# A dense two-layer block behind attention: eight of its nine remaining feature chunks go in pairs through seven block products in place of eight

## The chip, the cores and the metric

The program runs on one core of a Trainium2 chip. The metric is the device time of one execution in microseconds, the median of several runs. The names of the engines are those of the profile: PE (TensorE), DVE (VectorE), ACT (ScalarE), POOL (GpSimd), SP (SyncE, which here issues every DMA).

## The reference, cut to what matters

```python
scores = scale * np.matmul(q, k.transpose(0, 1, 3, 2))          # 8 x 8 heads, 576 tokens, 64 wide
thresh = np.max(scores, axis=-1, keepdims=True) - tau
scores = np.where(scores >= thresh, scores, -1000000000.0)
attn = np.exp(scores - np.max(scores, axis=-1, keepdims=True))
attn = attn / (np.sum(attn, axis=-1, keepdims=True) + 1e-09)
x = np.matmul(attn, v)              # turned to 4608 tokens x 512
h = x @ w_in                        # 512 -> 2048
g = np.maximum(h, 0.0) + alpha * np.minimum(h, 0.0)
out = g @ w_out                     # 2048 -> 512
```

w_in and w_out arrive as 64-bit floats; the kernel takes them apart on the chip.

## The kernel before, in words

Every float32 operand of a matmul is split in a rounded part ("h") and the rest ("l"), and a product is three matmuls: h by h, h by l, l by h. A split is one ScalarE copy (h) and one subtraction on GpSimd or VectorE (l).

The 2048 features are 16 chunks of 128. While attention runs, the first seven (F1 = 7) are decoded (`Split64`: ScalarE takes the size, VectorE shifts bits, GpSimd or VectorE joins the halves) and applied to groups of 256 tokens between attention's own matmuls; their second-layer sum goes to DRAM (`part`). Attention ends near 850 us. Then three things follow.

1. What is left of the first seven chunks, four groups of 256 tokens, named jobs j0 to j3. `first_layer` (tiles `phj`) does one chunk: 12 matmuls of 256 columns, then `prelu` on VectorE (L228, L229) and `split_g` (ACT L237, POOL L240) into `gj`. `second_layer` (tiles `accj`) does two blocks of 128 tokens with 21 matmuls of 512 columns each. x is split by `fetch_x` (ACT L835, POOL L836).
2. Chunks 7 to 10 for nine groups of 512 tokens, first layer and second layer, 12 and 12 matmuls of 512 columns per chunk and group; VectorE adds the sum to the residual loaded from `part` (L988, tiles `pinj`, `obj`) and it is written to `part` again.
3. Chunks 11 to 15 likewise, written to the output.

The order on an engine is that in which the code calls it (`manual_schedule`); `at_cycle` puts small work into numbered cycles between matmul groups, so that a decode or a split stands so many cycles ahead of its use. An engine runs its queue strictly in that order. PSUM has eight banks: four `ph` and four `acc`.

## Time and profile before

| what | value |
|---|---|
| median of three runs | 1378.01 us (1376.72 to 1378.1) |
| span of the profiled execution | 1374.2 us |
| PE busy | 1332.0 us (97%), 8116 matmuls |
| DVE / ACT / POOL busy | 72% / 61% / 60% |
| granted clock of PE, mean | 0.998 |
| DMA | 186.06 MB, mean 135 GB/s |

The profile is of one execution; its span runs from the first to the last instruction, and the time of a run has a few microseconds around it (1378.01 against 1374.2; the profiled execution's own run time isn't listed apart). Matmuls are pipelined, so their busy times overlap; distances between starts give their price. In a row by groups the columns are the line, the engine, the operation with the tiles written and read, the count, the busy time and mean in ns, then the engine's idle time ahead of them with what ended it.

### The profile page before, as it was taken

What the parts mean: (1) busy time and instruction counts of PE and PEld (TensorE: products, weight loads), DVE (VectorE), ACT (ScalarE), POOL (GpSimd) and SP (SyncE); (2) the same over time, 40 slices, a digit from 0 to 9 for tenths busy, and PEclk for the clock granted to TensorE, in tenths of its full rate; (3) what the DMA queues carried; (4) which work ended last, traced back from release to release, by engine and by line L of the source; (5) the groups of instructions that cost most, each with busy time, mean ns of one, the idle gap of its engine ahead of it and who ended that gap; (6) DMA issues with size and microseconds to landing.
All of it is one profiled execution on the core that took longest, in us unless ns stands there. A gap on an engine that the chain in (4) does not pass through costs nothing.

```text
span 1374.2 us, 24020 instructions
## 1 busy us (share of the span) xinstructions
PE 1332.0 (97%) x8116; PEld 1178.4 (86%) x8116; DVE 989.5 (72%) x1970; ACT 843.4 (61%) x1915; POOL 825.4 (60%) x949
## 2 busy tenths in 40 slices
PE   5988899999999999999999999999999999999998
PEld 4556789999999999999999998898888888888887
DVE  6999988889889889888888883873655644333432
ACT  6888888888888888888888873442323322211110
POOL 4886676576676666666666654884656554433431
PEclk9999999999999999999999999999999999999999
DMA  8643634644544545445445313445556352343222
GB/s 253 175 145 104 184 103 119 167 125 125 160 122 134 148 126 144 136 126 150 136 132 145 115 50 110 131 131 169 167 170 200 122 184 92 109 150 110 93 77 77
DMA packets 115179, 186.06 MB, mean 135 GB/s; under 512 B 18320, under 2 KB 49328, under 8 KB 115056
## 3 DMA queue, kind: packets, MB, share of 16 engines
q1 hardware_dynamic: 115056, 184.52, 45.0%
q8 instruction: 65, 1.06, 0.3%
q14 instruction: 58, 0.48, 0.1%
HBM read 104.41 MB, written 37.90 MB: 104 GB/s over the span
## 4 chain that ended last, share of the span: by engine, by line
PE 86%; ACT 5%; DVE 4%; issue 2%; POOL 2%; DMA 2%; SPq 0%; POOLq 0%; DVEq 0%; ACTq 0%
PE accj L246 19%; PE phj L210 18%; PE s L423 11%; PE av L570 11%; PE acca L246 9%; PE pha L210 9%; PE t L467 7%; PE tk L483 1%; DVE p L458 1%; DVE nmx L438 1%; DMA wri<-in_moe_w_in_dram 1%; ACT xb L583 1%; ACT p L446 1%; ACT xa L581 1%; ACT xh L196 1%
## 5 line engine op out<-in xcount | busy, mean ns | idle before, releaser
L240 POOL TENSOR_TENSOR gj<-ptj,gj 128x512 fp32r<-128x512 f32 (+1 forms) x109 | 129.2, 1187 | 237.2 <-ACT gj L237 236.5
L237 ACT ACTIVATE gj<-ptj 128x512 fp32r<-128x512 f32 (+1 forms) x109 | 62.9, 577 | 338.1 <-DVE ptj L229 338.0
L438 DVE TENSOR_REDUCE nmx<-s 128x1 f32<-128x576 f32 x288 | 217.2, 754 | 71.5 <-PE s L423 68.0
L246 PE MATMUL accj<-wo,gj 128*128 128x512 f32 x1140 | 262.4, 389 | 0.5 <-POOL gj L240 0.5
L246 PEld LDWEIGHTS accj<-wo,gj 128*128 128x128 f32 x1140 | 213.7, 188 | 45.3 <-POOL gj L240 1.0
L210 PE MATMUL phj<-xhj,wi 128*128 128x512 f32 (+1 forms) x816 | 232.7, 366 | 0.0
L458 DVE SCALAR_TENSOR_TENSOR p<-s,thr,p 128x576 f32<-128x576 f32 x256 | 206.9, 808 | 2.8 <-ACT thr L451 2.4
L446 ACT ACTIVATE p<-s,nmx 128x576 f32<-128x576 f32 x256 | 190.2, 743 | 8.2 <-DVE nmx L438 7.7
L246 PE MATMUL acca<-wo,ga 128*128 128x512 f32 x588 | 185.9, 422 | 1.6 <-POOL ga L240 0.8
L423 PE MATMUL s<-kh,qst 128*128 128x288 f32 x640 | 142.4, 313 | 33.6 <-DVE p L458 19.1
L210 PEld LDWEIGHTS phj<-xhj,wi 128*128 128x128 f32 x816 | 147.4, 188 | 25.4
L228 DVE TENSOR_SCALAR ptj<-phj,alpha_sb 128x512 f32<-128x512 f32 (+1 forms) x109 | 74.3, 681 | 124.1 <-PE phj L210 120.2
L210 PE MATMUL pha<-xh,wi 128*128 128x256 f32 x784 | 156.8, 283 | 0.2 <-ACT pra L223 0.2
L467 PE MATMUL t<-ident,p 128*128 128x128 f32 x1024 | 154.7, 274 | 0.0
L210 PE MATMUL phj<-xlj,wi 128*128 128x512 f32 (+1 forms) x408 | 149.8, 367 | 1.1 <-POOL xlj L836 0.9
L423 PEld LDWEIGHTS s<-kh,qst 128*128 128x128 f32 x640 | 101.4, 193 | 57.6 <-issue 25.1
L988 DVE TENSOR_TENSOR obj<-accj,pinj 128x512 f32<-128x512 f32 x72 | 49.8, 692 | 139.5 <-PE accj L246 118.5
L423 PE MATMUL s<-kl,qst 128*128 128x288 f32 x640 | 133.7, 299 | 0.0
L210 PEld LDWEIGHTS pha<-xh,wi 128*128 128x128 f32 x784 | 127.9, 190 | 4.5 <-ACT pra L223 1.5
L467 PEld LDWEIGHTS t<-ident,p 128*128 128x128 f32 x1024 | 126.5, 141 | 0.1
L233 POOL TENSOR_TENSOR pta<-pta,pra 128x256 f32<-128x256 f32 x94 | 69.4, 738 | 74.2 <-ACT pra L223 71.6
L246 PEld LDWEIGHTS acca<-wo,ga 128*128 128x128 f32 x588 | 102.0, 191 | 13.7 <-POOL ga L240 1.3
(130 smaller groups left out, 2867.3 us busy)
## 6 DMA issues: line engine op xcount, KB each, us to landing
pinj<-part SPq DMA_DIRECT2D x72, 256.0 KB
kr<-in_k_dram SPq DMA_DIRECT2D x31, 320.0 KB
rb<-rvd SPq DMA_DIRECT2D x64, 144.0 KB
xs<-xa SPq DMA_DIRECT2D x32, 288.0 KB
part<-obj SPq DMA_DIRECT2D x36, 256.0 KB
out_dram<-obj SPq DMA_DIRECT2D x36, 256.0 KB
vr<-in_v_dram SPq DMA_DIRECT2D x28, 320.0 KB
qr<-in_q_dram SPq DMA_DIRECT2D x31, 288.0 KB
```

The costliest lines, as they stand in the source:

```text
L210: nc.tensor.matmul(ph[:, :n], w[:, c, :], xx[:, c, :n], start=(c == 0 and ti == 0), stop=(c == NCC - 1 and ti == 2),)
L228: nc.vector.tensor_scalar(t[:, :n], ph[:, :n], 0.0, alpha_sb[:, fc : fc + 1], op0=ALU.min, op1=ALU.mult)
L233: nc.gpsimd.tensor_tensor(t[:, :n], t[:, :n], r[:, :n], op=ALU.add)
L237: nc.scalar.activation(g[:, 0, :n], t[:, :n], AF.Copy)
L240: nc.gpsimd.tensor_tensor(g[:, 1, :n], t[:, :n], f(g[:, 0, :n]), op=ALU.subtract)
L246: nc.tensor.matmul(acc[:m, :], gg[:, g, o : o + m], w, start=(first and ti == 0), stop=(last and ti == 2))
L423: nc.tensor.matmul(ps[:, h, :288], w, kk[:, a + h * 288 : a + (h + 1) * 288], start=(ki == 0 and i == 0), stop=(ki == 1 and i == n - 1),)
L438: nc.vector.tensor_reduce(self.nmx[:, j : j + 1], self.S[u][0][:, :, :288], axis=AX.XY, op=ALU.max, negate=True)
L446: nc.scalar.activation(pj, ps[:, :, :288], AF.Exp, bias=nmx[:, j : j + 1], scale=1.0)
L458: nc.vector.scalar_tensor_tensor(pj, ps[:, :, :288], thr[:, j : j + 1], pj, op0=ALU.is_ge, op1=ALU.mult, accum_out=self.sm[:, c : c + 1])
L467: nc.tensor.transpose(tb[:, c, :], pt[:, j, j * D + c * P : j * D + (c + 1) * P], ident)
L570: nc.tensor.matmul(pa[:m, :n], w, x, start=(part == 0 and c == 0), stop=(part == z.parts[-1] and c == NKC))
```

## The change

Chunk 7 stays as it is and becomes "the odd one". Chunks 8 to 15 become four pairs. For a pair, layer one is a 2 x 2 block product (two chunks by two halves of the 512 inputs, times two halves of the inputs by two stretches of 384 tokens), and layer two is one as well (two stretches of 256 tokens by the pair's two chunks, times two chunks by two halves of the 512 outputs). Each is done with seven products of sums of blocks in place of eight products of blocks. The products are numbered 1 to 7.

Layer one goes over all tokens first: six rounds s of 768 tokens, four pairs each, 24 units; a product is 6 matmuls of 384 columns (`product_a`). Sums of x blocks (`xt`, on GpSimd, in round 0 on VectorE) are split once per round; sums of w_in blocks once for all, decoded during part 1. Products 1, 6, 5 and 3 of a unit go to bank X, 7 and 4 to W, 2 to Y, so that a bank holds running sums: it is read between two products (`after_a`). Two chunks by two stretches come out, get the slope and go to DRAM (`gd`). The slope is applied as one maximum; chunks with a slope above one have their sign turned (`turn_sb`). Two units of a round carry the odd chunk's 12 matmuls right behind product 2 (`odd_a`).

Layer two then takes nine blocks s of 512 tokens: the gates of all chunks come back from DRAM, VectorE makes four sums and seven splits of 128 x 1024 columns (`gates_at`), and a product is 24 matmuls of 256 columns (`product_b`); the odd chunk's 24 are added in the same banks, one part in bank Z. `after_b` adds each product's bank to the residual `pin`, which is loaded 8 cycles ahead and lives in one of two memories by turns. w_out is decoded during layer one and its sums are split in the last four units (`weights_b`) into the places of the w_in sums. `turn_over` and `turn_again` give x's memory to the gates.

`ORDER` interleaves a unit's products with those of the unit before; `TURN` does it at the passage from layer one to layer two and `LAST` at the end.

```diff
-    fcs2 = list(range(F1, NF))
+    odd = F1
+    fcs2 = list(range(F1 + 1, NF))
...
+    ORDER = ((0, 1), (1, 5), (0, 7), (0, 2), (0, 6), (1, 3), (0, 4))
+    TURN = ((1, 5), (0, 1), (1, 3), (0, 7), (0, 2), (0, 6), (0, 4))
+    LAST = ((0, 1), (1, 5), (0, 7), (1, 3), (0, 6), (0, 2), (0, 5), (0, 4), (0, 3))
+    BANK = {1: "X", 6: "X", 5: "X", 3: "X", 7: "W", 4: "W", 2: "Y"}
...
+    USE = (1, 7, 2, 6, 4, 5, 3)
+    ODD = (0, 1)
...
+            def done(w):
+                if r == 0:
+                    w32[pr] = mem.lx.tile([P, 2, DM], F32, tag="w32", name=f"w32_{pr}", bufs=2)
+                nc.gpsimd.tensor_tensor(w32[pr][:, r], f(w.t), f(w.low), op=ALU.add)
...
+                tt(st[7], st[1], st[5], op=ALU.subtract)
+                tt(st[6], st[4], st[7], op=ALU.subtract)
...
+                tt(st[5], st[5], st[4], op=ALU.add)
+                tt(st[3], st[2], st[6], op=ALU.subtract)
...
+            at_cycle(c, temps)
+            for k, ns in enumerate(((1, 7, 2), (6, 4))):
+                for n in ns:
+                    at_cycle(c + k, hi, n)
+                    at_cycle(c + k + 1, lo, n, nc.gpsimd if n in (1, 2, 4) else nc.vector)
...
-        decode_part(parts2[0], i + 6, DEC2)
+        c = i + 5
+        for n in range(NJ):
+            first_word(n, c)
+            c += FW
+        odd_word("i", c, 4)
...
+                if k == (GB - F1 - 1 if final else 0) and num > 0 and not (num == 1 and pending.begun):
+                    second_layer(pending, mem.mp1)
...
+                    c += 1 if u < NA else 3
+                    if u < NA and prod == 2 and u % NP in ODD:
+                        steps.append((u, "o"))
+                        start[u, "o"] = c
+                        c += 1
...
+        def psum(u, prod):
+            b = BANK[prod]
+            fresh = prod in (1, 7, 2)
+            if fresh:
+                bank[u, b] = ps_3.tile([P, 512], F32, tag=b, name=f"p{b}{u}", bufs=3 if b == "X" else 2)
+            return bank[u, b], fresh
+
+        def product_a(u, prod):
+            s, pr = divmod(u, NP)
+            ph, fresh = psum(u, prod)
+            w = wsum[pr, prod]
+            xh, xl = xop[s, prod]
+            for c in range(2):
+                wh, wl = (w[:, k, c * P : (c + 1) * P] for k in range(2))
+                for ti, (a, x) in enumerate(((wh, xh), (wh, xl), (wl, xh))):
+                    nc.tensor.matmul(
+                        ph[:, :H1],
+                        a,
+                        x[:, c],
+                        start=(fresh and c == 0 and ti == 0),
+                        stop=(c == 1 and ti == 2),
+                        skip_group_check=not fresh,
...
+            for j, n in enumerate(((1, 2), ("o", 3))[ODD.index(pr)]):
+                xh, xl = xop[s, n]
...
+            if of is None:
+                g = mem.br.tile([P, H1], F32, tag="cr", name=f"cr{u}", bufs=2)
+                copy(g, ph, scale=turn_sb[:, col])
+                at_cycle(i + 1, larger, g, ph, slope_sb)
+            else:
+                g = sv.pop((u, of))
+                whole = ph
+                if prod == 5:
+                    whole = ps_3.tile([P, 512], F32, tag="Z", name=f"pZ{u}")[:, :H1]
+                stt(whole, ph, turn_sb[:, col], g, op0=ALU.mult, op1=ALU.add)
+                at_cycle(i + 1, copy, g, whole)
+                at_cycle(i + 2, larger, g, whole, alpha_sb)
...
+            at_cycle(need[1] - 8, load_pins)
...
+                c = need[n] - 6
+                if s == 0 and n == 2:
+                    c = start[NA - 1, 3] + 1
...
+        def product_b(u, prod):
+            acc, fresh = psum(u, prod)
+            s = u - NA
+            gh, gl = gop[s, prod]
+            todo = [(tb, pr) for tb in range(2) for pr in range(NP)]
+            for n, (tb, pr) in enumerate(todo):
+                wh, wl = (bsum[pr, prod][:, k] for k in range(2))
+                for ti, (g, w) in enumerate(((gh, wh), (gh, wl), (gl, wh))):
+                    nc.tensor.matmul(
+                        acc[:, tb * H2 : (tb + 1) * H2],
+                        g[:, pr, tb * P : (tb + 1) * P],
+                        w,
+                        start=(fresh and n == 0 and ti == 0),
+                        stop=(n == len(todo) - 1 and ti == 2),
+                        skip_group_check=not fresh,
+                    )
+                if n in (3, 6):
+                    cycle()
+            if prod == 7:
+                bank[u, "Z"] = ps_3.tile([P, 512], F32, tag="Z", name=f"pZ{u}")
+                odd_b(s, bank[u, "Z"], 1, 1, True)
+                at_cycle(i + 1, after_b, u, "o")
+            elif prod in (2, 3, 4):
+                odd_b(s, acc, *{2: (0, 0), 3: (0, 1), 4: (1, 0)}[prod], False)
...
+        def after_b(u, prod):
+            s = u - NA
+            acc = bank[u, "Z" if prod == "o" else BANK[prod]].rearrange("p (a m) -> p a m", a=2)
+            h, k = {1: (0, 0), 2: (0, 0), 6: (1, 0), 4: (1, 0), 7: (1, 1), 5: (1, 1), 3: (0, 1), "o": (1, 1)}[prod]
+            dst = pin[s, h][:, :, k * H2 : (k + 1) * H2]
+            nc.vector.tensor_tensor(dst, acc, dst, op=ALU.add)
+            if prod == (3 if h == 0 else 4 if start[u, 4] > start[u, 5] else 5):
+                t0 = G2 * s + H2 * h
+                nc.sync.dma_start(out[t0 : t0 + H2, :].rearrange("(a p) m -> p a m", p=P), pin[s, h])
```

The attention part keeps its instructions. Three places show how the queues change.

GpSimd's queue in part 1, at jobs j1 to j3. Before: gate splits (L240) and a joined weight word (L156) now and then.

```order
L240 TENSOR_TENSOR gj_1_12654<-ptj_1_12651,gj_1_12654 128x256
L240 TENSOR_TENSOR gj_2_12680<-ptj_2_12677,gj_2_12680 128x256
L156 TENSOR_TENSOR wi_12649<-wti_12588,wri_12499 128x512
L240 TENSOR_TENSOR gj_3_12701<-ptj_3_12698,gj_3_12701 128x256
L240 TENSOR_TENSOR gj_4_12721<-ptj_4_12718,gj_4_12721 128x256
L240 TENSOR_TENSOR gj_5_12741<-ptj_5_12738,gj_5_12741 128x256
L240 TENSOR_TENSOR gj_6_12763<-ptj_6_12760,gj_6_12763 128x256
L156 TENSOR_TENSOR wti_12672<-wti_12672,wi_12758 128x512
L240 TENSOR_TENSOR gj_0_12797<-ptj_0_12794,gj_0_12797 128x256
```

After, in the same part: gate splits (now L248) among the word's two steps (L849 rest, L975 join) and the splits of the weight sums (L861, `wa`).

```order
L248 TENSOR_TENSOR gj_4_13050<-ptj_4_13047,gj_4_13050 128x256
L861 TENSOR_TENSOR wa_1_13040<-w_2_12925,wa_1_13040 128x256
L861 TENSOR_TENSOR wa_2_13044<-w_2_12925,wa_2_13044 128x256
L248 TENSOR_TENSOR gj_5_13077<-ptj_5_13074,gj_5_13077 128x256
L861 TENSOR_TENSOR wa_4_13071<-w_2_12925,wa_4_13071 128x256
L248 TENSOR_TENSOR gj_6_13101<-ptj_6_13098,gj_6_13101 128x256
L849 TENSOR_TENSOR wri_12928<-wri_12928 128x512
L248 TENSOR_TENSOR gj_0_13128<-ptj_0_13125,gj_0_13128 128x256
L861 TENSOR_TENSOR wa_5_13117<-w_2_12925,wa_5_13117 128x256
L975 TENSOR_TENSOR w_3_13146<-wti_12991,wri_12928 128x512
```

Between two gate splits now stand up to two weight-sum splits or a word's step, where one word stood in four or five.

VectorE's queue in the same part. Before: activations of two lines per chunk (`ptj` from `phj`) and one step of a word.

```order
L228 TENSOR_SCALAR ptj_6_12760<-phj_6_12744,alpha_sb 128x256
L229 SCALAR_TENSOR_TENSOR ptj_6_12760<-phj_6_12744,ptj_6_12760 128x256
L156 TENSOR_TENSOR wri_12591<-wri_12591 128x512
L228 TENSOR_SCALAR ptj_0_12794<-phj_0_12766,alpha_sb 128x256
L229 SCALAR_TENSOR_TENSOR ptj_0_12794<-phj_0_12766,ptj_0_12794 128x256
L137 TENSOR_SCALAR wto_12781<-wto_12781 128x512
L140 TENSOR_SCALAR wto_12781<-wto_12781 128x512
```

After: the sums of w_in blocks (L993, L994), which read GpSimd's join `w`, stand ahead of a chunk's activation.

```order
L993 TENSOR_TENSOR sum_2_13036<-w_2_12925 128x256
L994 TENSOR_TENSOR sum_2_13037<-w_2_12925,sum_2_13036 128x256
L146 TENSOR_SCALAR wti_12991<-wti_12991 128x512
L236 TENSOR_SCALAR ptj_4_13047<-phj_4_13023,alpha_sb 128x256
L237 SCALAR_TENSOR_TENSOR ptj_4_13047<-phj_4_13023,ptj_4_13047 128x256
L861 TENSOR_TENSOR wa_7_13042<-sum_2_13036,wa_7_13042 128x256
L151 SCALAR_TENSOR_TENSOR wti_12991<-wri_12928,wti_12991 128x512
L236 TENSOR_SCALAR ptj_5_13074<-phj_5_13053,alpha_sb 128x256
L237 SCALAR_TENSOR_TENSOR ptj_5_13074<-phj_5_13053,ptj_5_13074 128x256
L861 TENSOR_TENSOR wa_6_13069<-sum_2_13037,wa_6_13069 128x256
```

The activation of chunk 4 (`ptj_4`) and with it the bank `phj` wait for GpSimd's word `w_2`.

VectorE's queue in the last 200 us. Before, a group of four chunks and its residual additions:

```order
L228 TENSOR_SCALAR ptj_14_15645<-phj_14_15632,alpha_sb 128x512
L229 SCALAR_TENSOR_TENSOR ptj_14_15645<-phj_14_15632,ptj_14_15645 128x512
L228 TENSOR_SCALAR ptj_15_15664<-phj_15_15651,alpha_sb 128x512
L229 SCALAR_TENSOR_TENSOR ptj_15_15664<-phj_15_15651,ptj_15_15664 128x512
L228 TENSOR_SCALAR ptj_11_15695<-phj_11_15670,alpha_sb 128x512
L229 SCALAR_TENSOR_TENSOR ptj_11_15695<-phj_11_15670,ptj_11_15695 128x512
L988 TENSOR_TENSOR obj_0_15717<-accj_0_15701,pinj_0_15586 128x512
L988 TENSOR_TENSOR obj_128_15742<-accj_128_15720,pinj_128_15588 128x512
```

After, half a block of layer two: residual additions (L1524, from banks X, W, Y, Z), splits (L861, `gl`), sums (L1439, L1447).

```order
L861 TENSOR_TENSOR gl_7_17350<-gt_7_17325,gh_7_17349 128x1024
L1524 TENSOR_TENSOR pin_0_17252<-pX_17336,pin_0_17252 128x2x256
L861 TENSOR_TENSOR gl_o<-go_17271,gh_o 128x512
L861 TENSOR_TENSOR gl_2_17382<-gr_01_17173,gh_2_17381 128x1024
L1439 TENSOR_TENSOR gt_6_17396<-gr_11_17186,gt_7_17325 128x1024
L1524 TENSOR_TENSOR pin_1_16993<-pX_17075,pin_1_16993 128x2x256
L861 TENSOR_TENSOR gl_6_17417<-gt_6_17396,gh_6_17416 128x1024
L1447 TENSOR_TENSOR gr_01_17173<-gr_01_17173,gt_6_17396 128x1024
L1524 TENSOR_TENSOR pin_1_17254<-pZ_17438,pin_1_17254 128x2x256
L1524 TENSOR_TENSOR pin_1_17254<-pW_17403,pin_1_17254 128x2x256
L861 TENSOR_TENSOR gl_3_17462<-gr_01_16912,gh_3_17461 128x1024
L1524 TENSOR_TENSOR pin_0_17252<-pY_17448,pin_0_17252 128x2x256
```

The activations are gone from there (they stand in layer one), and operand splits of 1024 columns stand behind additions that wait for a product.

More of the change, by code (lines that the diff above doesn't have):

```diff
@@ L27 @@
 G1 = 256
+H1 = 384
 G2 = 512
@@ L64 @@
 CYCLE = 2.6
+FW = 5
 def f(ap):
@@ new lines, in tile_masked_attention_moe @@
+        left[2].close()
+        mem.xr = pool(2, "xraw", "left")
+        others = x_at(0)
+        puts = second_layer(jobs[-1], mem.ws)
+        p1.close()
+        mem.xe = pool(6, "xe", "left")
+        mem.br = pool(3, "br", "right")
+        mem.pa = pool(4, "pa", "right")
+        others(puts)
+        start = {}
+        steps = []
+        c = i + 1
+        for n in range(NA + NB + 1):
+            for lag, prod in {NA: TURN, NA + NB - 1: LAST, NA + NB: ()}.get(n, ORDER):
+                u = n - lag
+                if 0 <= u < NA + NB:
+                    start[u, prod] = c
+                    steps.append((u, prod))
+                    c += 1 if u < NA else 3
[3 more added lines that the diff above has]
+                        c += 1
@@ new lines, in tile_masked_attention_moe @@
+        begin = start[0, 1]
+        end = c
+        place = {step: n for n, step in enumerate(step for step in steps if step[0] >= NA)}
+        left[5].close()
+        ps_3 = left[5].enter_context(tc.tile_pool(name="ps_3", bufs=1, space=PSUM, reuse_waits="tile"))
+        for s in range(1, NA // NP):
+            x_at(s)
+        bank = {}
+        def psum(u, prod):
[4 more added lines that the diff above has]
+            return bank[u, b], fresh
@@ new lines, in odd_a @@
+        def odd_a(u):
+            s, pr = divmod(u, NP)
+            ph = bank[u, "o"] = ps_3.tile([P, 512], F32, tag="Y", name=f"pO{u}", bufs=2)
+            wh, wl = (wi[odd][:, k].rearrange("p (c f) -> p c f", c=NCC) for k in range(2))
+            for j, n in enumerate(((1, 2), ("o", 3))[ODD.index(pr)]):
+                xh, xl = xop[s, n]
+                for c in range(2):
+                    for ti, (a, x) in enumerate(((wh, xh), (wh, xl), (wl, xh))):
+                        nc.tensor.matmul(
+                            ph[:, :H1],
+                            a[:, 2 * j + c],
+                            x[:, c],
+                            start=(j == 0 and c == 0 and ti == 0),
+                            stop=(j == 1 and c == 1 and ti == 2),
+                        )
@@ L1012, in tile_masked_attention_moe @@
+        for _ in range(3):
+            cycle()
+    for st in reversed(left):
         st.close()
```

440 lines of the change are left out of this document (372 added, 68 removed).

## Prediction

> **What bounds the kernel now.** I read the table by windows first, to see which engine is full in which stage behind attention (850 to 927: what is left of the first seven chunks; from there the nine others).
>
> ```profile
> core 0: us, PE busy (x) PEld busy (x) DVE busy (x) ACT busy (x) POOL busy (x), PEclk, DMA share, GB/s
> 850.00:927.00 77.00, 75.88 (x492) 68.95 (x491) 63.38 (x102) 37.35 (x80) 59.77 (x58) 1.00 0.44 137
> 927.00:1170.00 243.00, 243.00 (x1073) 201.18 (x1073) 125.52 (x187) 67.53 (x117) 137.00 (x104) 1.00 0.48 156
> 1170.00:1370.00 200.00, 199.46 (x881) 164.78 (x880) 70.54 (x100) 34.65 (x59) 75.17 (x59) 1.00 0.32 104
> ```
>
> From 927 on TensorE never stops, its granted clock is 1.00, and every other engine has a third of its time or more to spare. Only fewer or shorter matmuls shorten this part. Between 850 and 927 TensorE is also full, but VectorE has 82% and GpSimd 78% of the window busy: there the cover is thin. Next the price of one matmul, from starts in TensorE's timeline:
>
> ```profile
> 872.21 0.28 PE L210 MATMUL phj<-xhj,wi 128*128 128x256 f32 x1
> ...
> 882.01 9.71 PE L246 MATMUL accj<-wo,gj 128*128 128x512 f32 x42
> ...
> 922.05 9.71 PE L246 MATMUL accj<-wo,gj 128*128 128x512 f32 x42
> ...
> 1331.47 13.76 PE L246 MATMUL accj<-wo,gj 128*128 128x512 f32 x60
> 1345.07 0.39 PE L210 MATMUL phj<-xhj,wi 128*128 128x512 f32 x1
> ```
>
> Sixty matmuls of 512 columns start within 13.60 us: 226.7 ns each. Seven chunks of twelve with 256 columns lie between 872.21 and 882.01: 84 in 9.80 us, 116.7 ns. Each has its own weight load, and the load is hidden at both widths. 384 columns do not occur; halfway is 171.7 ns, which I take (170 by 512's price per column, 175 by 256's).
>
> **TensorE's work.** Nine chunks cost 9 x 9 x 12 = 972 matmuls in layer one and 36 x 9 x 3 = 972 in layer two: 1944 x 226.7 = 440.7 us. After: layer one has 24 units (6 stretches of 768 tokens, 4 pairs) of 7 products of 6 matmuls, 1008, and 12 x 12 = 144 for the ninth chunk, 1152 x 171.7 = 197.8 us. Layer two has 9 blocks of 7 x 24 plus 24, 1728 x 116.7 = 201.7 us. Together 399.5: **41.2 us less**. Seven blocks for eight would save a ninth of it, 49; the narrower matmuls give 8 back. By the Trainium skill (TensorE: Matmul & The Clock Gate, Back-to-back issue gap) a matmul takes N/2.4 + 2.5 ns; the saving would be 43.6 us, an estimate from that page; the rows show 7 to 11 ns more per matmul, so the trace disagrees.
>
> **What the cover costs.** The other engines get sums, splits and more evictions. Their prices, by groups (count | busy, mean ns) and GpSimd's first rows of that stage:
>
> ```profile
> L240 POOL TENSOR_TENSOR gj<-ptj,gj 128x512 fp32r<-128x512 f32 x81 | 105.5, 1302 | 219.0 <-ACT gj L237 219.0
> ...
> L240 POOL TENSOR_TENSOR gj<-ptj,gj 128x256 fp32r<-128x256 f32 x28 | 23.7, 852 | 18.3 <-ACT gj L237 17.5 <-DMA wri<-in_moe_w_in_dram 0.7
> ...
> L156 POOL TENSOR_TENSOR wi<-wti,wri 128x512 fp32r<-128x512 f32 x9 | 12.6, 1402 | 1.3 <-DVE wti L156 1.2
> ...
> L836 POOL TENSOR_TENSOR xlj<-xrj,xhj 128x256 fp32r<-128x256 f32 x12 | 10.8, 920 | 1.7 <-ACT xhj L835 1.6
> ...
> L229 DVE SCALAR_TENSOR_TENSOR ptj<-phj,ptj 128x512 f32<-128x512 f32 x81 | 56.0, 692 | 2.8
> ...
> L229 DVE SCALAR_TENSOR_TENSOR ptj<-phj,ptj 128x256 f32<-128x256 f32 x28 | 11.9, 425 | 1.0
> ...
> L145 DVE SCALAR_TENSOR_TENSOR wto<-wro,wto 128x512 int32<-128x512 int32 x9 | 9.9, 1101 | 0.1
> ...
> L156 DVE TENSOR_TENSOR wri<-wri 128x512 f32<-128x512 f32 x9 | 7.2, 805 | 0.0
> ...
> L988 DVE TENSOR_TENSOR obj<-accj,pinj 128x512 f32<-128x512 f32 x72 | 49.8, 692 | 139.5 <-PE accj L246 118.5 <-DMA out_dram<-obj 16.2 <-DMA pinj<-part 2.7
> ...
> L341 DVE TENSOR_TENSOR kl<-kr,kh 128x640 fp32r<-128x640 f32 x1 | 0.8, 825 | 0.0
> L341 DVE TENSOR_TENSOR kl<-kr,kh 128x576 fp32r<-128x576 f32 x1 | 0.8, 759 | 0.0
> ...
> L237 ACT ACTIVATE gj<-ptj 128x512 fp32r<-128x512 f32 x81 | 51.2, 632 | 311.6 <-DVE ptj L229 311.6
> ...
> L196 ACT ACTIVATE xh<-xr 128x1024 fp32r<-128x1024 f32 x1 | 1.0, 1046 | 0.0
> ...
> 852.44 0.73 POOL L240 TENSOR_TENSOR gj<-ptj,gj 128x256 fp32r<-128x256 f32 x1 [6.04 <-ACT gj L237]
> 853.88 0.74 POOL L240 TENSOR_TENSOR gj<-ptj,gj 128x256 fp32r<-128x256 f32 x1 [0.71 <-ACT gj L237]
> 855.32 0.73 POOL L240 TENSOR_TENSOR gj<-ptj,gj 128x256 fp32r<-128x256 f32 x1 [0.70 <-ACT gj L237]
> 856.77 0.75 POOL L240 TENSOR_TENSOR gj<-ptj,gj 128x256 fp32r<-128x256 f32 x1 [0.72 <-DMA wri<-in_moe_w_in_dram]
> ```
>
> *Seven chunks' remainder* (to 927). GpSimd now has 28 gate splits (0.85), 12 splits of x (0.92), 8 rests, 8 joins and 3 of the ninth chunk at 1.40, and 16 splits of weight sums at the 256-column price 0.85: 23.9 + 11.0 + 26.6 + 13.6 = 75.1 us, in order. From its first at 852.44, with the 2.1 us that it waits between the first four in any case, the last gate split ends at 929.6. TensorE wants it 18 matmuls into the last second layer. That one stands at 922.05, behind a first chunk of twelve (2.7 us) that no longer stands there: 919.3 + 4.1 = 923.4. So GpSimd is 6 us late without a wait in mid-queue; and there are such waits, since VectorE's sums stand behind GpSimd's join, the next chunks' activations behind the sums, and with four banks TensorE's next chunk behind those. At GpSimd's undisturbed 0.73 for a split and 1.3 for a word the total is 66 us and it is just in time: 0. With both queues waiting in turn, up to 18. I take **10**, nearest to the means of that window.
>
> *Into layer one's stage.* Its x loads (1.5 MB) stand behind the last first-layer chunk, under a second layer of 9.5 us (42 matmuls); at the 156 GB/s of the window above they take 9.8 us and product 1 needs only the first quarter, so that is about covered; product 4's split stands late in GpSimd's queue: 1.5 (0 to 4).
>
> *Layer one's stage.* A round (4 units, 768 tokens) gives TensorE 192 matmuls, 33.0 us. GpSimd: 20 half operands of 384 columns at 1.08 (between 0.85 and 1.30) and two words of 2.8, 27.4. VectorE: 30 evictions of 384 at 0.56, two sums at 0.96 (825 ns for 640 and 1.03 ns for each of 128 columns more), two words of some 3.1 (1.1 and 0.8 by L145 and L156, two shorter ones), 25. ScalarE: 30 copies at about 0.52 (632 ns for 512 columns), 8 splits of 768 at about 0.84 (half way to 1.05 for 1024), words, 25. All fit; in order, with three products (3.1 us) between an eviction and the next product in its bank. I take 4 us of waits in six rounds (0 to 12).
>
> *Turn to layer two.* Product 2's operand of the first block and the second block's loads can start only at layer one's last product, one 3.5 us product ahead of use: 2 (0 to 5).
>
> *Layer two's stage.* A block gives TensorE 192 matmuls, 22.4 us. VectorE: 7 splits and 4 sums of 1024 columns, each 825 + 384 x 1.03 = 1.22, 13.4; 8 additions at 0.69, 5.5; the ninth's split 0.7: 19.6, or 88%. The residual's tile is loaded only after the output of two blocks earlier has left it, so the block's first addition waits about 2.7 us by my count (19.7 us in, the write's 2.9, two 512 KB loads ahead of it, its own). What is queued behind on VectorE are operand splits with 2.6 us of slack. ScalarE has 8 us of work. DMA moves 4.5 MB a block, 199 GB/s, where the window above had 156 at a share of 0.48. I take 4 us for nine blocks (0 to 15).
>
> *The end.* The last addition was followed by a 256 KB write:
>
> ```profile
> 1370.61 0.69 DVE L988 TENSOR_TENSOR obj<-accj,pinj 128x512 f32<-128x512 f32 x1 [2.71 <-PE accj L246]
> 1371.33 0.33 SPq L990 DMA_DIRECT2D out_dram<-obj  x1
> ```
>
> 2.9 us from the issue to the span's end at 1374.2. Now it is 512 KB: 1.5 more (0 to 3).
>
> **Sum**: -41.2 + 10 + 1.5 + 4 + 2 + 4 + 1.5 = -18.2. The span of the profiled execution is 1374.2, the median of the runs 1378.01, so 3.8 us lie around the span and stay. 1356.0 span, **1360 us**. All lower ends: 1337; all upper: 1394.
>
> **Rivals.**
> *Everything is hidden* (0.22). The queues catch up, only the end and a few us remain: 1340. For it: 100% TensorE in the last two windows. Against: GpSimd's 75 us in a stage of 71.
>
> *VectorE becomes layer two's bound* (0.10), slower. If its 1024-column operations take twice L156's 805 ns, 1.61, a block is 17.7 + 5.5 + 0.8 = 24.0, and with the residual wait 26.7: 9 x 4.3 = 39 in place of 4, 1395. It turns slower when a block passes 22.4 + 22/9 = 24.8 us. For: 805 ns for 512 columns against 0.69 by the quiet rows. Against: GpSimd, which was busy beside L156, has nothing to do in that stage.
>
> *GpSimd becomes layer one's bound* (0.13). VectorE's operations on two SBUF operands (words' sign and join at 1.10 and 0.81, two sums at 0.96, weight sums 1) are 6.7 us of a round; if GpSimd stands still meanwhile its round is 34.1 against 33.0, and with 2.5 us of waits in order 36.6: 6 x 3.6 = 22 for 4, 1378; half of it, 1368. For: a 256-column split took 0.73 at 852.44 and 0.85 in the mean, beside VectorE's words. Against: most of VectorE's work there reads PSUM. By the Trainium skill (SBUF — State Buffer, Who interferes with whom) a VectorE operation with two SBUF inputs and a GpSimd one that reads SBUF exclude each other, the second waiting out the first; the trace's 0.73 against 0.85 agrees in kind.
>
> *Narrow matmuls cost more* (0.05), slower. If layer two's 256-column ones took 140 ns because of their loads, 1728 x 23.3 = 40: 1400. It decides at 129.4 (22 us over 1728). Against: the 84 in a row at 116.7; the most any row here shows is 120 (84 between 849.26 and 859.33).
>
> ```profile
> 849.26 0.28 PE L210 MATMUL phj<-xh,wi 128*128 128x256 f32 x1
> ...
> 859.33 0.28 PE L210 MATMUL phj<-xhj,wi 128*128 128x256 f32 x1
> ```
>
> **Numbers.** The forecast, TensorE bound with some 23 us of new waits, has 0.50, and by itself 1350 to 1370. Leaving out under 0.2 above and little below, the range is 1337 to 1382. About 0.2% (2.8 us) is what a measurement can tell here. Faster: 0.50 + 0.22 + most of GpSimd's 0.13 = 0.81; same 0.05 out of that case's upper end; slower 0.14.
>
> **What would show it.** Starts of layer-one products 1.03 us apart and of layer-two products 2.8 (with the ninth 3.5) show the price. TensorE's idle time behind GpSimd and VectorE between 860 and 940 shows the first term; idle time with VectorE as releaser in the last 200 us the fifth. I am wrong if layer one begins by 930, if a layer-two block takes over 24 us, or if the narrow matmuls' starts lie more than 125 ns apart.

## The result, and the profile after

The changed kernel takes 1391.35 us (median of four runs, 1391.04 to 1392.61), beside it the kernel before 1377.9: a ratio of 1.0105, 95% interval 1.0091 to 1.012. It is some 13 to 14 us slower, where the forecast was 18 us faster. Its profiled execution spans 1389.3 us.

TensorE does have less to do. Its timeline gives the two new prices by the starts of whole products, and the first and last start of each stage:

```profile
850.27 0.28 PE L218 MATMUL phj<-xh,wi 128*128 128x256 f32 x1
...
945.12 0.34 PE L1256 MATMUL pX<-xh,wa 128*128 128x384 f32 x1
...
979.22 0.34 PE L1256 MATMUL pX<-xh,wa 128*128 128x384 f32 x1
...
981.30 0.34 PE L1256 MATMUL pW<-xh,wa 128*128 128x384 f32 x1
...
1169.60 0.28 PE L1502 MATMUL pX<-wb,gh 128*128 128x256 f32 x1
...
1209.66 0.40 PE L1502 MATMUL pW<-wb,gh 128*128 128x256 f32 x2
...
1218.96 0.40 PE L1502 MATMUL pW<-wb,gh 128*128 128x256 f32 x2
...
1384.50 0.28 PE L1485 MATMUL pX<-wo,gl_o 128*128 128x256 f32 x1
```

Twelve matmuls of 384 columns start within 2.08 us, 173.3 ns each; 78 of 256 columns within 9.30 us, 119.2 ns. So the new work is 1152 x 173.3 + 1728 x 119.2 = 405.6 us, 35.1 less than before. Where the rest went stands in the windows of the three stages (remainder of the first seven chunks, layer one, layer two):

```profile
core 0: us, PE busy (x) PEld busy (x) DVE busy (x) ACT busy (x) POOL busy (x), PEclk, DMA share, GB/s
850.00:945.00 95.00, 85.29 (x506) 75.53 (x506) 70.69 (x122) 42.59 (x99) 73.37 (x79) 0.95 0.35 109
945.00:1170.00 225.00, 207.62 (x1152) 204.11 (x1151) 158.33 (x241) 139.76 (x265) 163.11 (x148) 0.96 0.49 159
1170.00:1389.00 219.00, 209.57 (x1733) 207.25 (x1731) 168.16 (x187) 72.53 (x81) 5.75 (x7) 1.00 0.56 174
```

TensorE is idle for 10 us in the first window and 17 in the second, where before it was busy almost throughout, and the granted clock is down to 0.95 and 0.96 in these two. TensorE's own waits, from 850 on, name who was late:

```profile
engine line waited for: us in total, times, longest us
PE pX L1256 <- ACT c L1306: 10.2, 3, 7.3
PE pX L1256 <- DVE pZ L1329: 8.1, 5, 2.9
PE phj L218 <- DVE ptj L237: 5.8, 3, 2.5
PE accj L254 <- POOL gj L248: 3.8, 2, 2.3
PE pX L1502 <- DVE gl L861: 2.2, 5, 0.5
```

The longest, 7.3 us, is in layer one's second round, and ScalarE, which is named, was not busy. Its cause is read backwards through the timelines of four engines:

```profile
964.28 0.69 PE L1256 MATMUL pX<-xh,wa 128*128 128x384 f32 x1 [7.27 <-ACT c L1306]
...
962.92 0.84 ACT L858 ACTIVATE xh<-xt 128x768 fp32r<-128x768 f32 x1 [8.08 <-POOL xt L1135]
...
960.94 1.94 POOL L1135 TENSOR_TENSOR xt<-xr,xr 128x384 f32<-128x384 f32 x2 [2.27 <-DMA xr<-xs]
...
956.80 0.37 SPq L1127 DMA_DIRECT2D xr<-xs  x1
```

TensorE waits for a copy out of a bank (`c`). The copy stands in ScalarE's queue behind the split of product 7's operand (`xh`), and that stands still 8.08 us for GpSimd's sum of x blocks, which stands for a load that was issued only at 956.80. The split is called 23 cycles ahead of its round; the copy was wanted at once.

The clock's part is seen in windows of 3.41 us, laid on the edges of the half-clock stretches:

```profile
core 0: us, PE busy (x), PEclk, DMA share, GB/s
863.36:866.77 3.41, 1.10 (x6) 1.00 0.55 161
866.77:870.18 3.41, 3.41 (x8) 0.50 0.33 99
...
955.52:958.93 3.41, 1.49 (x9) 1.00 0.80 242
958.93:962.34 3.41, 0.00 (x0) 0.50 0.31 104
...
1170.56:1173.98 3.42, 2.08 (x18) 1.00 0.73 231
1173.98:1177.39 3.41, 2.50 (x18) 1.00 0.41 135
```

A window in which TensorE is idle for 2.31 us (3.41 less 1.10) or 1.92 is followed by one at half clock; one with 1.33 us idle is not. Eight windows after 850 run at 0.50, three before layer one and five in it; TensorE is busy for 21.5 us of their 27.3, so they cost at most half of that, 10.7 us: where TensorE would have waited for another engine all the same, a slower matmul costs nothing. Before, no window after 850 did so until the last matmuls were over.

### The profile page after: what moved, and what is told of

Same layout as the page of the kernel before. It is cut to its first block, busy times and chain, and to the rows that moved or that the text cites. A ratio compares the mean times of both kernels' runs of the same rounds, so it can differ in the third digit from the quotient of the medians.

```text
span 1389.3 us, 26361 instructions
## 1 busy us (share of the span) xinstructions
PE 1314.6 (95%) x9052; PEld 1227.5 (88%) x9052; DVE 1128.8 (81%) x2134; ACT 957.3 (69%) x2103; POOL 795.8 (57%) x961
## 4 chain that ended last, share of the span: by engine, by line
PE 62%; DVE 12%; DMA 8%; ACT 7%; issue 5%; POOL 5%; SPq 1%; DVEq 0%; ACTq 0%; POOLq 0%
PE av L579 11%; PE s L432 11%; PE acca L254 9%; PE pha L218 9%; PE t L476 7%; PE pX L1256 4%; PE pX L1502 3%; PE pW L1256 2%; DMA pin<-part 2%; DMA out_dram<-pin 2%; DVE gl L861 2%; DVE pin L1524 1%; DVE p L467 1%; DMA xr<-xs 1%; DVE nmx L447 1%
## 5 line engine op out<-in xcount | busy, mean ns | idle before, releaser
L447 DVE TENSOR_REDUCE nmx<-s 128x1 f32<-128x576 f32 x288 | 217.2, 754 | 72.3 <-PE s L432 69.0
L1256 PE MATMUL pX<-xh,wa 128*128 128x384 f32 x384 | 110.3, 345 | 18.2 <-ACT c L1306 10.2
L218 PE MATMUL pha<-xl,wi 128*128 128x256 f32 x392 | 110.4, 282 | 0.0
L579 PE MATMUL av<-eo,vst 128*128 128x322 f32 (+1 forms) x512 | 107.3, 333 | 0.0
L1502 PE MATMUL pX<-wb,gh 128*128 128x256 f32 x576 | 104.2, 282 | 0.0
L532 DVE TENSOR_TENSOR eo<-t,eo 128x512 fp32r<-128x512 f32 (+1 forms) x168 | 97.4, 592 | 8.2 <-ACT eo L528 8.0
L432 PEld LDWEIGHTS s<-kl,qst 128*128 128x128 f32 x640 | 102.1, 191 | 0.0
L1256 PEld LDWEIGHTS pX<-xh,wa 128*128 128x128 f32 x384 | 71.9, 192 | 21.3 <-ACT c L1306 11.6
L1502 PEld LDWEIGHTS pX<-wb,gh 128*128 128x128 f32 x576 | 89.1, 190 | 0.0
L528 ACT ACTIVATE eo<-t 128x512 fp32r<-128x512 f32 (+1 forms) x168 | 84.7, 521 | 5.3 <-PE t L476 4.4
```

Source lines behind the costliest of these rows:

```text
L218: nc.tensor.matmul(ph[:, :n], w[:, c, :], xx[:, c, :n], start=(c == 0 and ti == 0), stop=(c == NCC - 1 and ti == 2),)
L432: nc.tensor.matmul(ps[:, h, :288], w, kk[:, a + h * 288 : a + (h + 1) * 288], start=(ki == 0 and i == 0), stop=(ki == 1 and i == n - 1),)
L447: nc.vector.tensor_reduce(self.nmx[:, j : j + 1], self.S[u][0][:, :, :288], axis=AX.XY, op=ALU.max, negate=True)
L528: nc.scalar.activation(dst[0], ps, AF.Copy)
L532: nc.vector.tensor_tensor(dst[1], ps, f(dst[0]), op=ALU.subtract)
L579: nc.tensor.matmul(pa[:m, :n], w, x, start=(part == 0 and c == 0), stop=(part == z.parts[-1] and c == NKC))
```

## The experiments

Two theories stood at the start. *Order*: the engines have the time, but in-order queues put work for later ahead of work that TensorE waits for. *Rate*: GpSimd and VectorE have too much to do, or slow each other, and moving it gains nothing. The stages are told apart by the starts of the first `phj`, `pX` and layer-two matmul and the last one. In profiles where a stage was not edited it varies: the remainder from 94.1 to 94.9 us, layer one from 222.8 to 224.5, layer two from 214.4 to 216.2. Less than 2 us of a stage is therefore not read; each stage time is of one profile, and the ratios are of all runs.

| kernel | ratio to before (95%) | remainder | layer one | layer two |
|---|---|---|---|---|
| changed kernel | 1.0105 (1.0091 to 1.012) | 94.9 | 224.5 | 214.9 |
| e1 split 7 later | 1.0055 (1.0041 to 1.007) | 94.7 | 217.2 | 214.4 |
| e2 two raw tiles | 1.0032 (1.002 to 1.0044) | 94.4 | 212.8 | 215.9 |
| e3 sums later | 1.0083 (1.0064 to 1.0103) | 93.4 | 222.8 | 215.6 |
| e4 third raw word | 1.0101 (1.0081 to 1.0122) | 96.0 | 222.7 | 216.2 |
| e5 no sums | 1.0043 (1.0029 to 1.0057) | 86.1 | 223.0 | 215.3 |
| e6 residual called earlier | 1.0097 (1.0072 to 1.0122) | 94.1 | 223.6 | 213.7 |
| e7 = e1 + e2 + e3 + start | 0.9961 (0.9944 to 0.9977) | 94.7 | 207.2 | 215.2 |
| e8 = e7 + clamp on VectorE | 0.9958 (0.9941 to 0.9975) | 93.2 | 204.9 | 215.5 |
| e9 = e8 + slope first | 0.9942 (0.9926 to 0.9959) | 93.1 | 206.1 | 214.9 |
| e10 = e9 + its split first | 0.9996 (0.9987 to 1.0005) | 98.4 | 205.8 | 214.9 |
| e11 = e8 + third residual | 0.9939 (0.9925 to 0.9954) | 93.7 | 207.8 | 210.1 |
| e12 = e11 + sum splits on VectorE | 0.993 (0.9912 to 0.9948) | 92.9 | 205.3 | 210.9 |
| e13 = e11 + sum splits on GpSimd | 0.9954 (0.994 to 0.9967) | 98.3 | 205.4 | 210.8 |
| e14 = e11 + words on VectorE | 0.9894 (0.9878 to 0.9909) | 88.9 | 205.5 | 210.9 |
| e15 = changed + words on VectorE | 1.0049 (1.0029 to 1.0068) | 86.8 | 223.5 | 215.8 |
| e16 = e12 + words on VectorE | 0.9876 (0.9853 to 0.9899) | 86.2 | 205.9 | 210.0 |

### Layer one: order

e1, ScalarE's split later:

```
-            for c, n in zip((-27, -22, -18, -15, -4, -2, 0), USE):
+            for c, n in zip((-27, -13, -18, -15, -4, -2, 0), USE):
```

> ScalarE's split of product 7's operand of x stands nine cycles later in its queue, 13 cycles ahead of use instead of 22. Theory A (queues in order: in the changed kernel ScalarE stands at that split for 8.08 us in round 1, because GpSimd waits for x from DRAM, and TensorE's bank copies stand behind it): the 7.27 us wait of TensorE at 957 to 964 falls under 2 us, the half-clock stretch of 10.2 us there shortens to 3.5 or goes, those near 1044 and 1082 go too; the time falls by 12 to 18 us, from 1391.4 to 1373-1379. Theory B (rate: GpSimd and VectorE have too much work and hinder each other, so the work comes late wherever it stands): the waits move to other lines and the time changes by less than 3 us.

e2, two of the four raw tiles doubled (`xr`, into which x is loaded before it is split):

```
-                    r = st[j, k] = mem.xr.tile([P, 2, H1], F32, tag=f"xr{j}{k}", name=f"xr{s}_{j}{k}")
+                    r = st[j, k] = mem.xr.tile([P, 2, H1], F32, tag=f"xr{j}{k}", name=f"xr{s}_{j}{k}", bufs=2 if k else 1)
```

> Two of the four raw tiles of x (second halves of the tokens) get a second buffer, so that a round's loads do not wait for the last splits of the round before. Theory A: GpSimd's waits for x (14.0 us, 5 times) and with them ScalarE's (16.2 us, 5 times) nearly go, TensorE's 7.27 us wait at 957 too; the time falls by 12 to 20 us to 1371-1379. Theory B: GpSimd is no earlier with its work, less than 3 us. Theory C (the loads themselves are slow, DMA being shared with the gates' and sums' writes): issue moves ahead by some 10 us, landing by less than half of it, and the gain is 3 to 8 us.

Both gained: by their ratios 0.5% (6.9 us) and 0.7% (10.1 us) of the changed kernel's time, all of it in layer one (7.3 and 11.7 us in the profiles). That is below what theory A had put on each, above B's 3, and for e2 above theory C's 3 to 8 as well. The waits of the stage tell why each alone is only a part. With e1 GpSimd still waits for x, but nobody stands behind ScalarE's split any more:

```profile
engine line waited for: us in total, times, longest us
POOL xt L1135 <- DMA xr<-xs: 14.7, 5, 4.3
PE pX L1256 <- DVE pZ L1329: 9.2, 8, 2.3
DVE xt L1132 <- POOL xt L1135: 6.7, 2, 5.2
PE pX L1256 <- ACT c L1306: 2.5, 2, 1.9
```

The 10.2 us of TensorE behind ScalarE are down to 2.5. VectorE's sum for product 6 now waits 6.7 us for GpSimd, and TensorE 9.2 us behind VectorE. With e2 GpSimd's wait for x is gone, and ScalarE stands once in round 1, for 5.8 us, behind six half splits in GpSimd's queue:

```profile
PE pX L1256 <- ACT c L1306: 6.4, 3, 3.5
ACT xh L858 <- POOL xt L1135: 5.8, 1, 5.8
PE pX L1256 <- DVE pZ L1329: 2.9, 3, 2.3
```

e7 puts e1, e2 and e3 (below) together and lets round 0's last splits wait until their products come near:

```
-                    for n in USE[1:]:
-                        if n == 4:
-                            sub4()
+                    for n in USE[1:4]:
                         hi(n)
                         lo(n)
                         if puts:
                             puts.pop(0)()
+                    sub4()
+                    for c, n in zip((3, 4, 7), USE[4:]):
+                        at_cycle(i + c, hi, n)
+                        at_cycle(i + c, lo, n)
```

> The first three edits together (product 7's split later, two raw tiles doubled, three pairs' sums later), and round 0's splits for products 4, 5 and 3 called in the cycles ahead of their use instead of before layer one's first product, so that ScalarE's first bank copies stand ahead of them. Alone the three gave 6.9, 10.0 and 3.0 us by their ratios; the first two share the wait of 7.27 us. Theory A (order): together 13 + 3, and the start's waits of 1.9 and 3.5 us with their half-clock stretch another 4 to 6: 18 to 23 us below the changed kernel, ratio to the kernel before 0.994 to 0.998. Theory B (rate): no more than 3 us below the better of the three, ratio 1.001 to 1.004.

It came out as order had it: 0.9961, below the kernel before, and 1.4% below the changed kernel, 20 us. Layer one takes 207.2 us in place of 224.5. The edit of round 0's splits was not run alone, so its share of this isn't known. The window is the proof against rate:

```profile
942.00:1150.00 208.00, 202.80 (x1153) 199.45 (x1152) 158.74 (x241) 140.06 (x265) 162.94 (x148) 1.00 0.51 168
```

VectorE is busy for 158.7 us, ScalarE for 140.1, GpSimd for 162.9: the same work as in the changed kernel's window of 225 us (158.3, 139.8 and 163.1), done in 17 us less, and the granted clock is 1.00 instead of 0.96.

e8 takes load from GpSimd there; the clamp of a w_out word (a maximum and a minimum in one operation) goes to VectorE:

```
-            w = Split64(mem.ws, ("w0", 2), mem.ws, ("w1", 2), "ppp", *src_o(fc))
+            w = Split64(mem.ws, ("w0", 2), mem.ws, ("w1", 2), "vpp", *src_o(fc))
```

> As the one before, and the clamp of the eight w_out words decoded during layer one is done on VectorE instead of GpSimd, where one takes 1.92 us. Theory A says GpSimd's queue is still what ScalarE's splits wait for: 2 to 4 us less than the one before. Theory B: GpSimd is no longer waited for, no change within 1.5 us. Theory C: VectorE's bank reads stand behind the clamps, 2 to 4 us more.

0.9958 against 0.9961: no difference that can be told. GpSimd is no longer what layer one waits for (theory B).

### Layer two: the residual's buffer

e6, an earlier call:

```
-            at_cycle(need[1] - 8, load_pins)
+            at_cycle(need[1] - 13, load_pins)
```

> The loads of the residual tiles are called 13 cycles ahead of a block of layer two in place of 8. VectorE's waits for them (27.8 us, 7 times, longest 4.9) fall below 8 us. Theory A (VectorE's splits behind these waits are what TensorE waits for in layer two): TensorE's waits for splits there (some 7 us in all) go, the time falls by 3 to 6 us. Theory B (VectorE makes the time up, and what is left is its own rate and the matmuls' price): within 1.5 us of the changed kernel.

It missed its own test: VectorE's waits for the residual stayed at 26.5 us, since each load still went out 2.7 us behind the write of the output from the same tile. e11 gives it another tile:

```
-                home = mem.b2 if s % 2 else mem.b1
+                home = mem.b2 if s % 3 == 1 else mem.b1
                 for h in range(2):
-                    t = pin[s, h] = home.tile([P, 2, DM], F32, tag=f"pin{h}", name=f"pin{s}_{h}")
+                    t = pin[s, h] = home.tile([P, 2, DM], F32, tag=f"pin{s % 3}{h}", name=f"pin{s}_{h}")
...
-            at_cycle(need[1] - 8, load_pins)
+            at_cycle(need[1] - 13, load_pins)
```

> On top of the kernel with the clamp on VectorE: the residual's tiles in layer two get a third buffer and their loads are called 13 cycles ahead. In the kernel with the earlier call alone the loads started at the same times as before (1226.0, 1238.3, 1249.5), each 2.7 us behind a write of the output from the same tile, so the buffer held them. Theory A (VectorE's waits for the residual, 26.5 us, delay its operand splits, for which TensorE waits): those waits fall below 6 us, TensorE's waits for splits in layer two go, layer two's 204.7 us shortens by 3 to 6. Theory B (VectorE catches up; TensorE is bound there by its own matmuls): VectorE's waits fall as well, but layer two shortens by under 1.5 us.

VectorE's waits in the changed kernel's layer two, and then in e11's:

```profile
DVE pin L1524 <- DMA pin<-part: 27.8, 7, 4.9
PE pX L1502 <- DVE gl L861: 2.2, 5, 0.5
PE pY L1502 <- DVE gl L861: 0.7, 3, 0.4
```

```profile
DVE pin L1526 <- PE pX L1504: 15.2, 15, 1.1
PE pY L1504 <- DVE gl L861: 0.4, 1, 0.4
```

No wait for a residual is left, VectorE waits for products, and layer two is 5.4 us shorter in the profile than e8's (210.1 for 215.5). By the ratios (0.9939 for 0.9958, intervals that overlap) the gain can't be told from nothing in e11 alone; the five later kernels of which four have the edit show 210.0 to 210.9, and e15, without it, 215.8.

### The remainder of the seven chunks: work on GpSimd and VectorE

Three edits of order there, and one that leaves the sums out. e3 moves three pairs' sums two cycles back, e4 gives the words a third raw buffer:

```
-                sums_at(c + 7, pr)
+                sums_at(c + (9 if pr < NP - 1 else 7), pr)
```

> The sums of w_in blocks for the first three pairs stand two cycles later, so that VectorE no longer reaches them before GpSimd has joined the word. Theory A: VectorE's waits for the joined word (3.2 us) go, and first-layer chunks of the remainder of the seven lose 3 to 6 us of bank waits: layer one begins at 939-942 instead of 945.1, the time is 1385-1388. Theory B: VectorE and GpSimd are busy with the same work at the same rate; layer one begins within 1.5 us of 945.1, the time is 1390-1393.

```
-            w = Split64(mem.ws, ("w0", 2), mem.ws, ("w1", 2), "vpp", *src_i(fcs2[n]))
+            w = Split64(mem.ws, ("w0", 3), mem.ws, ("w1", 2), "vpp", *src_i(fcs2[n]))
...
-            word_at(c, w, c - 4, done)
+            word_at(c, w, max(i, c - 6), done)
```

> The 64-bit words decoded behind attention get a third raw buffer and their loads are called two cycles earlier. Theory A: ScalarE's waits for words (6.1 us, longest 3.6) and VectorE's behind them (13.7 us, longest 7.7) fall to a third, the words' steps no longer stand bunched ahead of chunk activations, and layer one begins 3 to 6 us earlier: 1385-1388. Theory B: 1390-1393, the waits were free time that the same work fills elsewhere.

e3: 0.2% by the ratio, intervals that overlap, and 1.4 us of the remainder, within what it varies by; in e7 the stage is at 94.7 again. e4: nothing. e9 and e10 change what VectorE, ScalarE and GpSimd find first in a cycle:

```
             layer1_into(ph, fc, job.n, job.x["x"])
-            cycle()
             t = prelu(mem.mp1, G1, fc, job.n, ph, name, 2)
+            cycle()
```

> On top of the kernel before it (clamp on VectorE): behind attention, a first-layer chunk's two activation steps on VectorE are called ahead of the cycle's small work (words, sums) instead of behind it. Theory A (the order of VectorE's queue: a bank is freed only behind a run of word and sum steps): TensorE's waits for activations (phj) go, the gate splits come earlier, and the remainder of the seven chunks, 93.2 us there from its first first-layer matmul to layer one, falls by 4 to 9 us; ratio 0.989 to 0.993. Theory B (the small work is the bound, and now stands behind activations that wait for TensorE): it does not fall by more than 1.5 us, or grows.

> As the one before, and the gate's split too (ScalarE's copy, GpSimd's subtraction) is called ahead of the cycle's small work. Theory A for GpSimd's queue: its gate splits no longer stand behind weight-sum splits and word steps, TensorE's waits for gates (11 us in nine entries between 845 and 945 in the kernel with all four edits) fall by half, another 2 to 4 us less than the one before. Theory B: GpSimd now waits for ScalarE's copy of a gate ahead of work it could do, no gain or 1 to 4 us more.

e9 left the remainder where it was (93.1 for 93.2); e10, with `cycle()` behind `split_g` too, lengthened it to 98.4, more than its theory B had allowed. So these edits of order gave nothing here, against what had held in layer one. Less work did. e5:

```
-                tt(st[7], st[1], st[5], op=ALU.subtract)
-                tt(st[6], st[4], st[7], op=ALU.subtract)
+                st[7], st[6] = st[5], st[4]
...
-                tt(st[5], st[5], st[4], op=ALU.add)
-                tt(st[3], st[2], st[6], op=ALU.subtract)
```

> The four sums of w_in blocks per pair are left out (plain blocks are split and multiplied in their places, so the output is another one): 16 operations of 0.41 to 0.95 us fewer on VectorE behind attention, and no VectorE operation there that reads GpSimd's joined word or waits until GpSimd has split a block. Theory A1 (the sums, standing ahead of chunk activations, are what stretches the remainder of the seven chunks): the time from attention's last second-layer matmul to layer one, 95.1 us in the changed kernel, falls by 6 to 10 us, the time by as much. Theory A2 (the words' own steps and GpSimd's gate splits behind them stretch it): it falls by no more than 3 us.

The remainder fell to 86.1 us, 8.7 less, and the time by 0.6%, as theory A1 had it, with GpSimd's work as it was (72.9 us busy in the stage, 73.5 before) and VectorE's 7.6 us less; with the sums, VectorE's waits for GpSimd's word (3.2 us) are gone too. No window in it was at half clock any more (three of 3.41 us in the changed kernel, at most 5.1 us of the 8.7). The clock alone doesn't make this stage long: in e1, which leaves it as it was, one window ran at half clock instead of three, and the stage took as long.

```profile
core 0: us, PE busy (x), PEclk, DMA share, GB/s
850.99:945.69 94.70, 82.47 (x505) 0.98 0.35 108
```

TensorE was idle there for 12.2 us, where the changed kernel had 9.7: what the clock didn't take, the waits did. Whose work it is was asked by moving it. e12, e13 and e14 start from e11:

```
e12
-                    at_cycle(c + k + 1, lo, n, nc.gpsimd if n in (1, 2, 4) else nc.vector)
+                    at_cycle(c + k + 1, lo, n, nc.vector)
...
-                at_cycle(c + 4, lo, n, nc.gpsimd if n == 5 else nc.vector)
+                at_cycle(c + 4, lo, n, nc.vector)
e13: the same two lines with nc.gpsimd
e14
-                nc.gpsimd.tensor_tensor(w32[pr][:, r], f(w.t), f(w.low), op=ALU.add)
+                nc.vector.tensor_tensor(w32[pr][:, r], f(w.t), f(w.low), op=ALU.add)
...
-            w = Split64(mem.ws, ("w0", 2), mem.ws, ("w1", 2), "vpp", *src_i(fcs2[n]))
+            w = Split64(mem.ws, ("w0", 2), mem.ws, ("w1", 2), "vvp", *src_i(fcs2[n]))
```

> On top of the kernel with the third residual buffer: the 16 splits of weight sums that GpSimd does behind attention (0.81 to 0.93 us each) go to VectorE, which takes 0.42 us for one when GpSimd reads nothing and up to 0.96 beside it. Theory G (GpSimd's queue is the bound of the remainder of the seven chunks, since the gate splits for which TensorE waits stand in it): from 93.7 us the remainder falls by 4 to 8. Theory D (VectorE's queue is the bound: activations stand behind the small work): it grows by 2 to 6. Theory S (the two share their way to SBUF, and only the sum of their two-operand work counts): it falls by 2 to 5, since VectorE needs half GpSimd's time for the same split.

> On the same base the other way: all 28 splits of weight sums on GpSimd, 12 more than before. Theory G: the remainder grows by 5 to 9 us. Theory D: it falls by 2 to 5. Theory S: it grows by 2 to 5.

> On the same base: the words' rests and joins (16 on GpSimd, 1.11 and 1.35 us) are done on VectorE, where two such of before took 0.81 us. Theory G: the remainder falls by 5 to 10 us. Theory D: it grows by 5 to 10. Theory S: the sum of two-operand time falls by some 16 x 0.4 us, the remainder by 3 to 6.

More on GpSimd: 98.3. Less on GpSimd: 92.9 and 88.9, from e11's 93.7. VectorE as the only bound had the other sign for e13 and e14 and is out. Of the sizes, sharing foretold e13 and e14 (4.6 more, 4.8 less) and neither theory e12's 0.8, with 14 us less of GpSimd's work. By the ratios e14 is faster than e11 clear of noise, and e12 and e13 can't be told from it; in e13 four windows of the stage ran at half clock and in e11 two, so part of its 4.6 us may be the clock. Then e14's edit alone on the changed kernel, and e12's and e14's together:

> The changed kernel with one edit: the w_in words' rests and joins on VectorE instead of GpSimd, nothing else. Theory G/S (GpSimd's work, slowed by VectorE's two-operand operations, is the bound of the remainder of the seven chunks): the remainder falls from 94.9 to 89 to 91 and the time by 4 to 6 us, ratio 1.0060 to 1.0080. Theory O (it helps only once VectorE's queue has been put in order by the later sums): less than 2 us.

> On top of the words on VectorE (with all edits before it): the 16 weight-sum splits on VectorE as well, which then has some 88 us of work in a stage of 89, GpSimd 41. Theory G: the remainder falls by another 2 to 5 us from 88.9. Theory S with VectorE full: it stays within 1 us or grows by up to 4, since VectorE is now the bound; ratio 0.989 to 0.992.

GpSimd's groups between 850 and 945 in the changed kernel, and the word steps in e15:

```profile
L248 POOL TENSOR_TENSOR gj<-ptj,gj 128x256 fp32r<-128x256 f32 x28 | 22.0, 789 | 18.7 <-ACT gj L245 18.6
L861 POOL TENSOR_TENSOR wa<-w,wa 128x256 fp32r<-128x256 f32 x16 | 13.7, 866 | 1.2 <-ACT wa L858 1.1
L975 POOL TENSOR_TENSOR w<-wti,wri 128x512 f32<-128x512 f32 x8 | 10.8, 1352 | 0.2
L849 POOL TENSOR_TENSOR wri<-wri 128x512 f32<-128x512 f32 x8 | 8.9, 1110 | 0.7 <-DVE wri L156 0.7
```

```profile
L849 DVE TENSOR_TENSOR wri<-wri 128x512 f32<-128x512 f32 x8 | 6.5, 809 | 0.1
L975 DVE TENSOR_TENSOR w<-wti,wri 128x512 f32<-128x512 f32 x8 | 5.9, 740 | 0.1
PEld accj L254 <- POOL gj L248: 2.3, 4, 1.1
```

The words' 19.7 us on GpSimd become 12.4 on VectorE, TensorE's weight loads wait 2.3 us for gates (5.2 before), and the remainder falls by 8.0 us to 86.8, more than any theory had put on it. All three of its half-clock windows are gone with the gaps; that is at most 5.1 of the 8. TensorE's wait for VectorE's activations stays (5.3 us, 5.8 before). In e16 VectorE has 79.4 us of work in the window of 86 from 850 on and GpSimd 41.8, and the remainder is at 86.2: 2.7 below e14, as theory G had it, though the intervals of the two ratios overlap and the stage has one half-clock window instead of two. VectorE at 92% did not become the bound that theory S expected.

e16 is the fastest kernel: 1360.14 us, a ratio of 0.9876 (0.9853 to 0.9899) to the kernel before, with every product of the change still in it.

## Why the prediction was wrong, step by step

**TensorE's work** was put at 41.2 us less and is 35.1 less. The step that failed is taking 116.7 ns for 256 columns from seven clean chunks; of the two figures quoted (116.7, and 120 over the first 84) the later one was nearer: 78 matmuls of layer two in a row had 119.2, which is 4.3 us over 1728. 384 columns took 173.3 instead of 171.7 ns, another 1.8. Narrow matmuls as a rival needed 129.4 ns, and did not come.

**The remainder** was put at 10 us (0 to 18). The same matmuls took 79.6 us in the kernel before (from 849.26 to 931.60, less 2.7 for the twelve of chunk 7), and 94.85 now: 15.2. In the kernel before, the first matmul behind the remainder was:

```profile
931.60 0.39 PE L210 MATMUL phj<-xhj,wi 128*128 128x512 f32 x1
```

The mechanism was named: TensorE waits for gates from GpSimd (3.8 us) and for activations from VectorE, in whose queue the sums stand (5.8 us), and less work on either side (e14 and e15, e5) shortens the stage. The size was not: 10 was a choice between 0 and 18, and the measured 15.2 lies nearer to the case of both queues waiting in turn. GpSimd's time alone, by which the text reckoned its 6 us, does not set the stage (e12 took 14 us of it away for 0.8, e5 none of it for 8.7); how the rest divides between the two queues stays open. The 75 us forecast for GpSimd are 73.4 in the window, 5.4 of them for layer one's first operands.

**Into layer one and layer one's stage** are the steps that failed: 1.5 and 4 us, with 16 at the most, against 25.9 (224.5 us for 1146 matmuls of 173.3 ns before the first of layer two). The work was counted rightly (all fit in a round), and the split of product 4 was feared for; what the text did not do is ask in which cycle each small step is *called*, and what then stands behind it. Product 7's split is called 23 cycles ahead of the round and stands ahead of bank copies; its data are behind a raw tile that the round before frees last; and round 0's splits stand ahead of the first bank copies. e1, e2 and e7 show this: e7 gives 17.3 of the 25.9 us back. At most 5.6 of the 25.9 is the clock in five windows. What is left in e7, 8.6 us, was not taken apart.

**Turn and layer two** were put at 2 and 4, and measured 7.9 (214.9 for 1728 matmuls of 119.2 ns and six left of layer one). The late residual is what the forecast named, and e11, which frees VectorE of it, is 5.4 us shorter in that stage. **The end**: 1.5 forecast; the last matmul stands 4.8 us before the end, 4.0 before the change, so 0.7.

The sum: -35.1 + 15.2 + 25.9 + 7.9 + 0.7, and 1.0 that the remainder began later (850.27 against 849.26), is 15.6; the spans differ by 15.1. The medians differ by less, 13.45, because the forecast's 3.8 us around the span was wrong too: the profiled run of the changed kernel took 1391.04 us with a span of 1389.3, so 1.7 lie around it; by the same 1.7 the profiled execution of the kernel before was some 2 us shorter than the median of its runs.

**The rivals.** Everything hidden is refuted by TensorE's 27 us of idle time in the two stages. GpSimd as layer one's bound (0.13) is refuted by e7 and e8: the same 163 us of GpSimd's work fit in 208. VectorE as layer two's bound needed 24.8 us a block; the nine blocks took 214.9, 23.9 each, and the operations of 1024 columns took 1.22 us as estimated. None of the rivals had the mechanism that decided: waits in order of more than 16 us in layer one, with a slower clock behind them. None of the signs named in advance spoke: layer one began after 930 (at 945.1), a layer-two block took under 24 us, the narrow starts lay under 125 ns apart. They watched for the rivals, and none watched layer one's own waits: it is the only stage whose idle time no sign asked for, and none asked for the clock.

## What to carry to other kernels

For every small operation that a change adds to an in-order queue, ask what the operation waits for when its turn comes, and who stands behind it; an engine with 30% to spare can still cost TensorE 7 us if one copy stands behind a split that is called early. A forecast of waits also needs the clock: where waits gathered to 2 us within one window of 3.41, the next window ran at half speed; whether that costs time depends on who is waited for then. And where neither order nor buffers move a stage, move the work to the other engine, both ways, before believing in either as the bound.
